# A planner's DMA rates changed: 320 bytes per ns for large rows, 180 for transposes

## The chip, the core and the metric

One core of a Trainium2 chip runs the whole program in one launch. The metric is the device time of one execution in microseconds, as the median of several runs; one execution is also recorded by the hardware profiler.

## What is computed

Attention with a block-causal mask, a dense layer with an ELU, and a mixture of experts with one expert per token:

```python
scores = 1 / sqrt(64) * q @ k.T                  # batch 4, 8 heads, 576 rows, 64 columns
scores = where(row // 64 >= column // 64, scores, -1e9)
x = softmax(scores) @ v                          # regrouped to 2304 tokens x 512
h = x @ w_in                                     # 512 x 2048
x = elu(h) @ w_out                               # 2048 x 512
out = x.copy()                                   # experts: 8, of 512 x 1024 and 1024 x 512
xc = x[x @ w_skip > 0]                           # the other tokens keep x
e = argmax(xc @ w_gate); gate = softmax(xc @ w_gate)[e]
out[those] = xc + gate * (relu(xc @ w1[e]) @ w2[e])
```

## The kernel before

All matrix products that need more precision than one half-precision pass are done as three passes over a high and a low half (f16). The first two chunks of the dense layer use f32 weights that arrive in shuffled form and are rebuilt on VectorE.

**Attention** goes batch by batch (4), in groups of 64-row blocks, by head pairs (4), each row block a unit with five steps: `s_unit` (scores on TensorE), `x_unit` (row maxima on VectorE, exponentials on ScalarE), `h_unit` and `l_unit` (high and low half of the normalised weights, tile `ehl`), and a transpose of `ehl` into `et`, which `pv` multiplies with v on TensorE. The transposes are DMAs issued by SyncE, except for the first two blocks of the first batch, which TensorE transposes (`turn`). `prep_k` and `prep_q` split raw k and q rows and transpose them by DMA into `kt` and `qt`; q is also copied with its halves swapped (`qt<-qt`).

**The dense layer** runs over 9 chunks of 256 tokens (`l1`, `l1a`, `l1b`, `l2`). Its weights come as 32 pieces of 512 KB (`raw_load`, tile `rw`), each rebuilt by three VectorE instructions (`conv`, tiles `twi`, `two`). `post` writes each 128-token tile to the output and to a DRAM scratch `pay_d`, and transposes it by DMA (`x2t`) for the router (`logits`, `route`, `route2`).

**The experts**: weight loads (`load_w`) start when the attention has left its memory (`leave_attention`). They are charged by `rc.call("sp", 0.48, load, [], [pl.key], 1.46, also=left)`, that is with a constant. Tokens are gathered from `pay_d` by GpSimd and transposed by a SyncE DMA (`gather`).

**The order.** Nothing is issued while the program is written down. `Recorder` keeps every instruction as a step with a cost (`_Engine.cost`: busy time on its engine, and for SyncE a second number, the transfer time) and its dependences. `Recorder.order` then plays the whole program through, step by step, on modelled engines, and `issue` emits the instructions in the order of the modelled start times. Of the candidates that are ready on an engine at the earliest time, the one with the lowest record number (`steps[i][3]`) is taken. The modelled times go nowhere else: the chip's engines run their own lists in order and wait on semaphores. One plan reaches from the first load up to the experts; each expert's first tokens and the last ones have small plans of their own, with the same costs. The DMA is one server in the model:

```python
if e == "sp":
    f = max(f, dma_free - 3.0)
...
if e == "sp":
    if len(lanes) >= 8:
        t = max(t, lanes[-8])
    end = max(t + (1.12 if s[1] < 0.6 else 1.3), dma_free) + s[2]
    dma_free = end
    lanes.append(end + 0.9)
    free[e] = t + s[1]
```

Here `s[1]` is SyncE's own issue time and `s[2]` the transfer time; a step that depends on a transfer starts 1.0 us after `end` at the earliest (`LAT["sp"]`).

Of the kernel before, what the change touches and what calls it, by code (L numbers as in the profile page):

```python
# [270 lines left out]
def _count(ap):  # L271
    n = 1
    for _, c in ap:
        n *= c
    return n
# [15 lines left out]
class _Engine:  # L291
# [21 lines left out]
    def cost(self, op, k):  # L313
        e = self.e
        out = k["out"]
        if e == "sp":
            b = _count(out.ap) * mybir.dt.size(out.dtype)
            if op == "dma_start_transpose":
                return max(1.2, b / 290e3 + 0.35), b / 290e3
            run = min(a.ap[-1][1] * mybir.dt.size(a.dtype) for a in (out, k["in_"]))  # L320
            return 0.48, b / 360e3 * (2 if run < 512 else 1)
        n = _count(out.ap[1:])
        sb = all(x.space == bass.MemoryType.SB for x in (out, k.get("in_", out), k.get("in0", out)))
        if e == "pe":
            if op == "transpose":
                return (0.2 if out.dtype == F32 else 0.06), 0.0
            t = n / 2400.0 * (4 if k["lhsT"].dtype == F32 else 1)
            here = out.offset // out.ap[0][0]
            prev, self.rec.last_pe = self.rec.last_pe, here
            return (0.02 if prev == 0 and here == 64 and n < 400 else max(t, 0.01)), 0.0  # L330
        if e == "act":
            aps = any(hasattr(k.get(x), "tensor") for x in ("scale", "bias"))
            return (0.094 if sb else 0.051) + n * 0.833e-3 + 0.093 * (aps + ("accum_out" in k)), 0.0
        if e == "dve":
            if op == "tensor_reduce":
                n = _count(k["in_"].ap[1:])
            aps = any(hasattr(k.get(x), "tensor") for x in ("scalar", "scalar1", "scalar2"))
            x = 1.0
            if op in ("tensor_copy", "tensor_scalar") and sb:
                x = 0.5 if mybir.dt.size(k.get("in_", k.get("in0")).dtype) == 4 else 0.25  # L340
            return 0.069 + n * x / 960.0 + 0.061 * aps, 0.0
        if op == "indirect_dma_start":
            return 1.05, 2.0
        return 0.15, 0.0
# [1602 lines left out]
```

## Time and profile before

| | us |
|---|---|
| median of 3 runs (lowest, highest) | 741.16 (740.03, 742.42) |
| the profiled execution | 738.97 |
| its span on the core | 737.0 |

The profiler records one execution. Busy times are sums over an engine's instructions within the span; a wait is idle time of an engine before an instruction, put down to what released it last. The DMA share is the mean busy share of the core's 16 DMA engines, and can exceed 1 a little. Line L310 is the helper through which all recorded instructions pass, so groups are told apart by their tiles: `out<-in`. PE is TensorE, DVE VectorE, ACT ScalarE, POOL GpSimd, SP or SPq SyncE's queue.

### The profile page before, as it was taken

How to read it: one execution, taken by the hardware profiler on the slowest of the kernel's cores; microseconds unless marked ns; L12 is line 12 of the kernel's file. 1: busy time of each engine (PE TensorE's matmuls, PEld its weight loads, DVE VectorE, ACT ScalarE, POOL GpSimd, SP SyncE). 2: the span in 40 equal slices, each digit the busy share in tenths (PEclk: the TensorE clock that was granted, in tenths of full speed). 3: DMA queues.
4: the chain of work that ended last, by engine and by line, in shares of the span. 5: the costliest groups of instructions: out<-in, count | busy, mean ns of one | idle time of the engine just before them, and what ended most of it. 6: DMA issues, size and time to landing. Idle time of an engine off the chain costs nothing. (4 is left out here: it accounts for less than half of the span.)

```text
span 737.0 us, 17736 instructions
## 1 busy us (share of the span) xinstructions
PE 675.2 (92%) x6665; PEld 464.0 (63%) x6665; DVE 576.2 (78%) x1664; ACT 511.8 (69%) x1090; POOL 84.9 (12%) x122
## 2 busy tenths in 40 slices
PE   4677988999999999989999999999999999998894
PEld 3456633775466666647656667657576777676683
DVE  5897999887999999878969955999688645555662
ACT  5976746899887888667758745766466548585682
POOL 2000000001000100100100000100105034243311
PEclk9989999999999999999999999999999999999998
DMA  9999999799696999899638449826164786999941
GB/s 265 232 260 312 272 285 259 167 166 164 120 194 139 186 179 192 148 177 185 111 66 162 89 70 256 316 78 209 44 200 145 210 173 130 234 240 259 260 131 16
DMA packets 263259, 134.52 MB, mean 183 GB/s; under 512 B 234539, under 2 KB 235573, under 8 KB 262640
## 3 DMA queue, kind: packets, MB, share of 16 engines
q1 hardware_dynamic: 258960, 125.69, 75.0%
q0 software_dynamic: 4192, 7.49, 4.9%
q8 instruction: 57, 0.93, 0.5%
q14 instruction: 50, 0.41, 0.2%
HBM read 74.38 MB, written 12.75 MB: 118 GB/s over the span
## 5 line engine op out<-in xcount | busy, mean ns | idle before, releaser
L310 PE MATMUL h<-xt,win 128*128 128x256 f16 x1344 | 158.5, 273 | 1.6 <-DVE n L310 1.0
L310 PE MATMUL y<-wout,g 128*128 128x512 f16 x672 | 156.5, 381 | 0.0
L310 PEld LDWEIGHTS <-win 128*128 128x128 f16 x1344 | 128.9, 98 | 25.1 <-issue 2.8
L310 PEld LDWEIGHTS <-g 128*128 128x128 f16 x672 | 64.4, 98 | 67.3 <-issue 1.3
L310 ACT ACTIVATE e<-s,mx 128x512 f32<-128x512 f32 (+4 forms) x160 | 82.4, 517 | 26.6 <-DVE mx L310 11.3
L310 ACT ACTIVATE ehl<-e,su 128x512 f16<-128x512 f32 (+4 forms) x160 | 80.5, 550 | 22.4 <-DVE su L310 10.5
L310 DVE SCALAR_TENSOR_TENSOR ehl<-e,su,ehl 128x512 f16<-128x512 f32 (+4 forms) x160 | 81.9, 536 | 10.5 <-ACT ehl L310 10.3
L310 DVE TENSOR_REDUCE mx<-s 128x1 f32<-128x512 f32 (+4 forms) x160 | 74.5, 474 | 6.1 <-PE s L310 5.7
L310 PE MATMUL s<-kt,qt 128*128 128x384 f16 (+5 forms) x384 | 70.1, 310 | 9.9 <-ACT e L310 6.3
L310 PE MATMUL h<-xt,twi 128*128 128x256 f32 x256 | 59.4, 383 | 3.9 <-DVE g L310 2.4
L310 PE MATMUL y<-two,g 128*128 128x512 f32 x128 | 61.3, 618 | 1.3 <-DVE two L310 1.3
L310 PE MATMUL xps<-et,vt 128*64 128x128 f16 (+1 forms) x1440 | 49.5, 218 | 13.8 <-DVE xt L310 2.8
L310 PEld LDWEIGHTS <-vt 128*64 128x64 f16 x1440 | 39.9, 113 | 32.2 <-issue 23.8
L310 ACT ACTIVATE el<-h,col 128x512 f32<-128x512 f32 x56 | 38.2, 682 | 24.5 <-PE h L310 23.6
L310 PEld LDWEIGHTS h<-xt,twi 128*128 128x128 f32 x256 | 47.4, 190 | 10.8 <-DVE g L310 3.0
L310 PEld LDWEIGHTS <-p 128*128 128x128 f16 x984 | 47.0, 99 | 10.2 <-issue 4.1
L310 ACT ACTIVATE g<-el,col 128x512 f16<-128x512 f32 x56 | 40.1, 718 | 18.4 <-DVE el L310 17.9
L310 PEld LDWEIGHTS <-qt 128*128 128x128 f16 (+1 forms) x384 | 28.8, 105 | 28.8 <-issue 11.1
L310 DVE SCALAR_TENSOR_TENSOR g<-el,col,g 128x512 f16<-128x512 f32 x56 | 41.7, 744 | 3.8 <-ACT g L310 3.7
L1506 DVE SCALAR_TENSOR_TENSOR p<-p,n,p 128x1024 f16<-128x1024 f32 x32 | 40.7, 1279 | 4.7 <-ACT p L1505 4.5
L310 DVE SCALAR_TENSOR_TENSOR el<-h,col,el 128x512 f32<-128x512 f32 x56 | 41.7, 745 | 1.3
L310 PEld LDWEIGHTS <-hh 128*64 128x64 f16 (+1 forms) x432 | 28.5, 106 | 19.6 <-DVE hh L310 2.6
(233 smaller groups left out, 1132.3 us busy)
## 6 DMA issues: line engine op xcount, KB each, us to landing
p<-in_moe_w_dram SPq DMA_DIRECT2D x49, 512.0 KB, 5.8
rw<-in_moe_w_in_dram SPq DMA_DIRECT2D x16, 512.0 KB, 7.0
rw<-in_moe_w_out_dram SPq DMA_DIRECT2D x16, 512.0 KB, 5.4
pb<-in_moe_w_dram SPq DMA_DIRECT2D x10, 512.0 KB, 4.5
vflat<-in_v_dram SPq DMA_DIRECT2D x4, 1152.0 KB, 10.2
out_dram<-pay SPq DMA_DIRECT2D x18, 256.0 KB, 2.7
pay_d<-pay SPq DMA_DIRECT2D x18, 256.0 KB, 2.6
raw<-in_k_dram SPq DMA_DIRECT2D x16, 256.0 KB, 4.8
```

The lines of the kernel that those rows point to most:

```text
L310: rec.call(e, time, lambda: getattr(self.real, op)(*args, **kw), reads, writes, dma)
L1506: rc.call("dve", 1.2, lambda: nc.vector.scalar_tensor_tensor(out=half(1), in0=raw.t, scalar=sc, in1=half(0), op0=ALU.mult, op1=ALU.subtrac ...
```

## The change

In `_Engine.cost` the transfer time of a DMA transpose is its bytes at 180 bytes per ns, where it was 290; SyncE's own issue time of the transpose keeps the 290. Another transfer is charged at 320 bytes per ns, where it was 360, if its innermost runs have at least 512 bytes, and at 180, as before, if they are shorter. The constant 1.46 of the expert weights stays.

```diff
@@ -316,9 +316,9 @@
         if e == "sp":
             b = _count(out.ap) * mybir.dt.size(out.dtype)
             if op == "dma_start_transpose":
-                return max(1.2, b / 290e3 + 0.35), b / 290e3
+                return max(1.2, b / 290e3 + 0.35), b / 180e3
             run = min(a.ap[-1][1] * mybir.dt.size(a.dtype) for a in (out, k["in_"]))
-            return 0.48, b / 360e3 * (2 if run < 512 else 1)
+            return 0.48, b / (180e3 if run < 512 else 320e3)
         n = _count(out.ap[1:])
```

## Rows read from the trace of the kernel before

**Rows 1.** The page, part 1: busy time, share of the span, instructions.

```profile
PE 675.2 (92%) x6665; PEld 464.0 (63%) x6665; DVE 576.2 (78%) x1664; ACT 511.8 (69%) x1090; POOL 84.9 (12%) x122
```

**Rows 2.** Stretches: length, busy time (instructions) by engine, PE clock, DMA share, GB/s.

```profile
20.00:140.00 120.00, 98.92 (x691) 62.85 (x690) 107.49 (x287) 82.94 (x189) 1.17 (x5) 0.96 1.04 258
140.00:448.00 308.00, 299.68 (x2989) 199.36 (x2988) 263.29 (x828) 237.60 (x582) 16.77 (x25) 0.99 0.82 148
448.00:600.00 152.00, 150.21 (x1227) 103.93 (x1226) 124.43 (x370) 93.13 (x144) 21.33 (x26) 1.00 0.61 181
600.00:737.00 137.00, 117.30 (x1684) 91.53 (x1681) 70.92 (x151) 86.35 (x158) 41.88 (x28) 0.97 0.76 184
```

**Rows 3.** Stretches of the head: PE, PEld, DVE, ACT, POOL busy; clock, DMA share.

```profile
80.00:100.00 20.00, 18.09 (x101) 9.79 (x100) 20.00 (x44) 13.55 (x28) 0.00 (x0) 1.00 1.16 291
40.00:140.00 100.00, 85.94 (x574) 53.65 (x570) 88.65 (x229) 64.17 (x139) 1.17 (x5) 0.96 1.06 263
```

**Rows 4.** DMA issues, 0 to 140 us: count, KB each, median us to landing.

```profile
rw<-in_moe_w_in_dram SPq DMA_DIRECT2D x16, 512.0 KB, 7.0
...
et<-ehl SPq DMA_TRANSPOSE x11, 5.7
```

**Rows 5.** DMA queues (packets, MB, share) and issues, 408 to 446 us.

```profile
q1 hardware_dynamic: 10540, 2.64, 38.5%
...
et<-ehl SPq DMA_TRANSPOSE x6, 4.3
```

**Rows 6.** Two stretches with loads of expert weights; last columns DMA share, GB/s.

```profile
449.00:453.00 4.00, 4.00 (x41) 3.58 (x40) 2.37 (x6) 1.84 (x3) 0.00 (x0) 1.00 1.01 331
461.00:470.00 9.00, 9.00 (x72) 6.45 (x71) 8.91 (x30) 4.85 (x9) 0.00 (x0) 1.00 1.04 398
```

**Rows 7.** Waits of VectorE, 0 to 140 us: us in total, times, longest.

```profile
DVE twi L310 <- DMA rw<-in_moe_w_in_dram: 6.6, 6, 3.4
...
DVE two L310 <- DMA rw<-in_moe_w_out_dram: 1.5, 2, 1.1
```

**Rows 8.** Timeline of VectorE: start, us, instruction, [idle before it].

```profile
9.21 0.43 DVE L310 TENSOR_SCALAR twi<-rw 128x512 int32<-128x512 int32 x1 [1.02 <-DMA rw<-in_moe_w_in_dram]
...
60.48 0.43 DVE L310 TENSOR_SCALAR twi<-rw 128x512 int32<-128x512 int32 x1 [3.35 <-DMA rw<-in_moe_w_in_dram]
...
61.55 0.68 DVE L310 SCALAR_TENSOR_TENSOR g<-g,h 128x512 f32<-128x512 f32 x1
...
62.75 0.68 DVE L310 SCALAR_TENSOR_TENSOR k<-raw,k 128x512 f16<-128x512 f32 x1
```

**Rows 9.** Waits, 40 to 80 us.

```profile
DVE twi L310 <- DMA rw<-in_moe_w_in_dram: 5.2, 4, 3.4
```

**Rows 10.** Timeline of TensorE behind the wait of 3.35 us.

```profile
62.28 3.72 PE L310 MATMUL h<-xt,twi 128*128 128x256 f32 x16 [0.92 <-DVE g L310]
```

**Rows 11.** Waits of TensorE, 0 to 140 us.

```profile
PE s L310 <- DMA qt<-qt: 1.4, 1, 1.4
```

**Rows 12.** Waits of TensorE, 140 to 600 us.

```profile
PE xps L310 <- DMA et<-ehl: 2.3, 4, 1.1
...
PE s L310 <- DMA qt<-qt: 0.4, 1, 0.4
```

**Rows 13.** Waits of SyncE's queue, 0 to 140 us.

```profile
SPq L310 <- DVE mx L310: 6.5, 3, 5.3
```

**Rows 14.** Waits of TensorE, 600 to 740 us.

```profile
PE hp L310 <- ACTq L1787: 5.7, 4, 2.9
```

**Rows 15.** DMA issues of the whole span, gathers' transposes.

```profile
mxwo<-gp SPq DMA_TRANSPOSE x10, 5.7
```

**Rows 16.** Timeline of TensorE, the last product of attention weights and v.

```profile
446.90 0.86 PE L310 MATMUL xps<-et,vt 128*64 128x128 f16 x24
```

**Rows 17.** Timeline of SyncE, the first loads of expert weights.

```profile
448.97 1.49 SPq L1455 DMA_DIRECT2D p<-in_moe_w_dram  x3
```

**Rows 18.** Stretch in which the experts' weights are prepared.

```profile
520.00:600.00 80.00, 79.19 (x667) 53.69 (x666) 57.94 (x204) 45.28 (x74) 19.14 (x24) 1.00 0.58 155
```

## The prediction

> **What bounds the kernel now.** I read the page first for the engines' shares: TensorE is busy 675.2 of 737.0 us [rows 1], so 61.8 us of idle TensorE is all that a new order can win back. The table of stretches then says where that idle time lies [rows 2]: 20 to 140 us has 120 - 98.92 = 21.1, 140 to 448 has 8.3, 448 to 600 has 1.8, and the experts behind 600 have 19.7 (the rest, about 11, lies before 20 us). From 140 to 600 us the kernel is simply TensorE's work laid end to end. In the first 140 us three things are short at once: from 40 to 140 us VectorE is busy 88.65 of 100 and the DMA share is 1.06, and in the fullest slice, 80 to 100, they stand at 20.00 of 20 and 1.16 [rows 3]. The last places to look were the waits and the DMA rows, because this change touches nothing but the planner's idea of when a transfer ends.
>
> **What the change can and cannot do.** It adds and removes no instruction. The planner writes an order for each engine; its times are thrown away. So a cost matters only where it makes one engine, SyncE among them, take two steps in another order. Three prices move. A transpose goes from bytes/290 to bytes/180: a 256 KB one from 0.90 to 1.46 us, a 512 KB one from 1.81 to 2.91. A large row goes from 360 to 320: a 512 KB piece of the first two weight matrices from 1.46 to 1.64, an 1152 KB block of v from 3.28 to 3.69, a 256 KB write from 0.73 to 0.82. Small rows stay (360/2 is 180). SyncE's own issue time of a transpose, the fixed latencies, the 3 us of backlog, and the 1.46 us which the expert weights carry as a constant all stay.
>
> **Are the new prices nearer to the chip?** I added up what the planner charges for the transfers of a stretch and set it beside the DMA share times the stretch. For 140 to 448 us: transposed attention weights of three batches, 12 head pairs of 1.64 MB, 67.8 us before and 109.2 after; transposes of q and k, 7.08 MB, 24.4 and 39.3; swapped copies of q, 3.5 MB, 9.8 and 11.1; raw q, k, v, 10.6 MB of small rows, 59.0 both; some nine output tiles with a transpose and two writes each, 21.2 and 27.8. The sums are 182 and 246 us. The chip's DMA was busy 0.82 x 308 = 253 us there [rows 2]. For 20 to 140 us, with the counts of that stretch, two of them in [rows 4], less what was issued before 20: 27 weight pieces 39.3 and 44.2, three blocks of v 9.8 and 11.1, raw rows 20.4 both, the transposes 24.6 and 39.6, the small rest about 5.5 both. That is 99.6 and 120.8, against 1.04 x 120 = 125 on the chip [rows 2]. So the old plan believed that a sixth of the DMA was free in the head and 40% in the attention; the new plan sees about what the trace has. A stretch that moved almost nothing but transposes confirms the price: 2.64 MB at 38.5% of 38 us [rows 5] is 180 GB/s of busy time. Its six transposes of attention weights average some 0.40 MB (one 256 KB transpose is in the sum beside them) and landed in a median of 4.3 us [rows 5]; the planner's sum of latency, transfer and hand-over gives 1.3 + 1.37 + 1.0 = 3.7 before and 4.5 after. For large rows the trace is less clear: 398 GB/s at share 1.04 in one stretch, 331 at 1.01 in another [rows 6], so 328 to 383 at a full share, and 320 is low rather than high.
>
> [...]
>
> **The gain, term by term.** What can be won are stalls of an engine at a step that the old plan put too early.
>
> (a) VectorE at pieces of the first weight matrix, 6.6 us in six waits in 0 to 140 us and 1.5 in two at the second matrix [rows 7]. Of the 6.6, 5.2 in four waits lies in 40 to 80 us [rows 9], the largest of them 3.35, which ends at 60.48 [rows 8]; the rest, the larger wait 1.02 of it [rows 8], stands before 10 us, where nothing else is at hand. Behind the 3.35 VectorE had an activation, started at 61.55 [rows 8], for which TensorE waited 0.92 us [rows 10], and a raw k, split at 62.75 [rows 8]; whether either was ready by 57 the rows don't say. Winnable: 5.2 + 1.5 = 6.7 at most, zero at least, because the DMA is full there and the piece comes no sooner. With VectorE busy 88.65 of 100 us a filled stall is worth something, but not all of it reaches TensorE: I take a quarter, 1.7.
>
> (b) TensorE itself at a transfer: 1.4 at swapped q before 140 us [rows 11], then 2.3 at transposed attention weights and 0.4 at swapped q [rows 12], 4.1 in all. A matrix product that stands behind can go first; I take a little under half, 1.9, between zero and the whole.
>
> (c) SyncE, in order too, stops at a transpose whose data is not there, and the loads behind it wait: in 0 to 140 us the waits for the row maxima alone are 6.5 us in three, the longest 5.3 [rows 13]. The change shifts which transfer stands at such a place, and I can't tell to which side: bounds -5.3 to +5.3, the longest single wait, value 0.
>
> (d) The experts have plans of their own, and their gathers' transposes get dearer too. Those stand in SyncE's queue beside weight loads with unchanged cost and are for tokens of the next expert; what ends TensorE's waits there is an engine's branch, 5.7 us in four, not a transfer [rows 14]. Value 0; if loads slip behind such transposes, 0.56 us for each of ten that the longest row counts [rows 15] is a bound of 5.6 on the slow side.
>
> (e) The end of attention at about 447.7 (the last product of attention weights and v starts at 446.90 [rows 16]) releases the memory for the expert weights, whose loads begin two us later, at 448.97 [rows 17]. If the new plan, which charges 64 us more of DMA to the attention, ends it later, the preparation of the experts starts later. From 520 to 600 VectorE, which prepares them, is busy 57.94 of 80 us [rows 18]: 22 us of room. So a slip of a few us costs nothing; without that cover it costs its full length.
>
> Sum: 1.7 + 1.9 = 3.6. The profiled execution took 738.97, its span 737.0; the median of the runs shown is 741.16. I count from the median: **741.16 - 3.6 = 737.5 us**. From the profiled run alone it would be 735.4.
>
> **Rivals.**
> *Same (0.33).* The order changes, the stalls only move. For it: TensorE's waits at transfers are 4.1 us of 61.8, and the head has VectorE, DMA and activations all full, so that reordering leaves each sum as it is. Against it: the old plan is wrong by a sixth in the head, and 3.35 us of VectorE's idle time stands there in one piece. Time: 739 to 743.
> *Slower, by the weight pieces (0.25).* With 0.18 us more for each of 16 pieces of the first matrix, 0.41 for each of three blocks of v and 0.56 for six transposes of q and k, the plan believes the last piece to come 16 x 0.18 + 3 x 0.41 + 6 x 0.56 = 7.5 us later. VectorE then does softmax first, the converted weights come late, and TensorE, which has only attention beside them, stands idle. It decides where the pieces land before the plan's time; rows 6 with 383 GB/s speak for that, the share of 1.06 over 40 to 140 us [rows 3] against it. Half of 7.5 lost gives 745, all of it 748.7.
> *Slower, because transposes are quick (0.05).* If they ran like the large loads of rows 6, the products that use them would stand up to 1.1 us too late in 12 head pairs, 13 us at the end of attention, of which (e) hides most: 742 to 748. [...]
> *Faster (0.37)*, the forecast, 734 to 739. All stalls of (a) and (b) gone would be 6.7 + 4.1 = 10.8: 730.4.
>
> About 2.2 us, 0.3%, is what a measurement here can tell from no change. Faster 0.37, same 0.33, slower 0.30. The range that leaves out no more than 2 in 10 runs from 730, every stall won, to 748, the slow rival nearly whole; the forecast's own is 734 to 739.
>
> **What would show it.** Right: the same number of instructions on each engine; VectorE's wait at weight pieces between 40 and 80 us under 3 us instead of 5.2; TensorE's waits at transfers under 3 instead of 4.1; TensorE's idle time in 20 to 140 us at 18 or less; no more of it from 140 to 600. Wrong: the first product with converted weights clearly later than before and TensorE's idle in the head at 24 or more (the slow rival), or idle time that appears between 448 and 600, or behind 600, where I put nothing: then an order that I held to be covered was not.

## The result and the profile after

The changed kernel takes 748.49 us in the median of six runs (745.74 to 753.53) against 741.79 for the kernel before, measured beside it (six runs, 736.24 to 745.17): a ratio of **1.0141, 95% interval 1.0099 to 1.0182**. This ratio, like every one below, is an estimate over the fast executions (those more than 1.5% above the kernel's fastest are left out) and not the quotient of the two medians beside it, which is 1.0090 here and below differs from the ratio by up to 0.003. Either way the kernel is slower. The forecast was 737.5, and the measured median lies half a microsecond above the top of its range.

The profiled execution took 749.83 us, its span is 748.1, 11.1 more than before. First the page of the changed kernel, part 1:

```profile
PE 682.1 (91%) x6665; PEld 467.0 (62%) x6665; DVE 579.1 (77%) x1664; ACT 510.3 (68%) x1090; POOL 82.9 (11%) x122
```

The instruction counts are those of [rows 1]. TensorE is busy 6.9 us longer and idle 4.2 us longer. The stretches of the changed kernel, with the columns of [rows 2]:

```profile
20.00:140.00 120.00, 98.02 (x611) 63.14 (x610) 107.20 (x283) 80.53 (x183) 0.97 (x4) 0.88 1.02 252
140.00:448.00 308.00, 303.60 (x3054) 200.80 (x3053) 265.82 (x833) 237.16 (x586) 16.31 (x26) 1.00 0.80 152
448.00:600.00 152.00, 145.61 (x1161) 98.44 (x1160) 120.11 (x356) 91.32 (x138) 17.84 (x24) 0.98 0.54 168
```

The granted clock from 20 to 140 us is 0.88 (was 0.96), and from 0 to 20 it was 0.81 (was 1.00); the 256 products `h<-xt,twi` of the dense layer's first chunks take 402 ns in the mean, where they took 383.

Against [rows 2], TensorE's idle time is 22.0 us (was 21.1) from 20 to 140, 4.4 (was 8.3) from 140 to 448, and 6.4 (was 1.8) from 448 to 600. From 140 to 448 TensorE has fewer gaps; the stretch behind it, where nothing was expected, lost 4.6 us. Two milestones, the groups of the attention's last products and of the first products of an expert block (minimum, median and longest duration in ns, first and last start in us), show the same in time:

```profile
L310 PE MATMUL xps<-et,vt x1440: 189/219/316, 21.4 to 449.3; 128*64 128x128 f16 x129, 128*64 128x64 f16 x51
...
L1128 PE MATMUL ahp<-mxt,p x192: 216/219/219, 582.4 to 604.4; 128*128 128x128 f16 x192
```

Before, they start at 447.5 (the group of [rows 16]) and 576.2. So the changed kernel is 1.8 us late at the attention's end, 6.2 late at the first expert block, and 11.1 late at the end.

**What stands between 449 and 582.** The waits of the changed kernel (total, times, longest), whole span:

```profile
PE ns L310 <- DVE cb L310: 4.2, 1, 4.2
...
DVE li L310 <- DMA lst_d<-li,si: 8.1, 4, 5.2
```

And its timeline over the place (start, duration, engine and instruction, [idle before it]):

```profile
454.52 1.83 SPq L1455 DMA_DIRECT2D p<-in_moe_w_dram  x4
456.39 2.07 SPq L1458 DMA_DIRECT2D p<-in_moe_w_dram  x4
458.51 4.42 SPq L1455 DMA_DIRECT2D p<-in_moe_w_dram  x4
463.97 5.25 SPq L1458 DMA_DIRECT2D p<-in_moe_w_dram  x4
...
465.32 0.97 POOL L310 DMA_INDIRECT lst_d<-li,si  x1 [41.43 <-DVE li L310]
471.39 0.97 POOL L310 DMA_INDIRECT lst_d<-li,si  x1 [5.10 <-DMA lst_d<-li,si]
...
470.38 1.21 DVE L1475 TENSOR_REDUCE n<-p 128x1 f32<-128x1024 f32 x1
476.79 0.17 DVE L310 COPY li<-tokid 128x2 f32<-128x2 f32 x1 [5.20 <-DMA lst_d<-li,si]
...
477.83 0.16 DVE L310 CAST cb<-n 128x1 bf16<-128x1 f32 x1
...
478.04 0.16 PE L310 MATMUL ns<-cb,ones 128*128 128x1 bf16 x1 [4.16 <-DVE cb L310]
478.07 5.28 PE L310 MATMUL y<-wout,g 128*128 128x512 f16 x12
```

Read it from the bottom. TensorE stood still 4.16 us for `ns`, a product of 0.16 us that waits for the small tile `cb`. VectorE makes `cb`, and VectorE stood still 5.20 us at a copy of 0.17 us: token numbers into `li`, the buffer of the router's list. `li` is a ring of two, and the buffer was still being read by an indirect scatter into `lst_d`, which GpSimd had issued at 471.39. That scatter and the one ahead of it moved among sixteen 512 KB loads of expert weights, issued from 454.52 to 469.2, and took 5.3 and 5.8 us to land, against a median of 2.8 for all sixteen scatters before. The token numbers don't depend on anything: the planner put the copy far ahead of the gate value that goes into the same buffer, and on an engine in order that makes everything behind it wait for the scatter. Before, the same loads began at 448.97 [rows 17], and the scatters came when they were nearly over; they landed in 2.8 and 2.1 us. GpSimd's timeline of the kernel before:

```profile
474.65 1.22 POOL L310 DMA_INDIRECT lst_d<-li,si  x1 [48.61 <-DVE li L310]
477.67 0.97 POOL L310 DMA_INDIRECT lst_d<-li,si  x1 [1.79 <-DMA lst_d<-li,si]
```

That the loads are what makes the scatter slow is read from these two orders; no run changed the loads alone.

The wait costs twice: twelve `y` products take 2.75 us three times between 457 and 472 of the changed kernel, and 5.28 behind the stall. In 478 to 484 the granted clock is 0.56, after it was 1.00 in 455 to 470. Stretches of the changed kernel:

```profile
455.00:470.00 15.00, 15.00 (x123) 10.51 (x122) 12.89 (x48) 9.46 (x17) 0.97 (x1) 1.00 1.01 383
470.00:478.00 8.00, 3.88 (x30) 2.84 (x29) 2.76 (x12) 2.42 (x4) 0.97 (x1) 0.90 0.97 364
478.00:484.00 6.00, 5.96 (x21) 2.56 (x21) 6.00 (x11) 5.83 (x7) 0.00 (x0) 0.56 0.01 5
```

**Behind 582.** In GpSimd's queue of the changed kernel the scatter of an expert block's result went ahead of the three gathers for the next tokens:

```profile
597.93 1.68 POOL L1168 DMA_INDIRECT out_dram<-o,ah  x1 [7.91 <-DVE lists L310]
599.91 1.10 POOL L310 DMA_INDIRECT gp<-pay_d,lists  x1 [0.31 <-DVE mv L310]
```

Before, the gathers went first:

```profile
590.07 1.18 POOL L310 DMA_INDIRECT gp<-pay_d,lists  x1 [8.42 <-DVE lists L310]
...
596.61 1.65 POOL L1168 DMA_INDIRECT out_dram<-o,ah  x1 [2.49 <-issue]
```

The second expert's first product then waits 4.17 us for a branch where it waited 1.07. TensorE's timeline of the changed kernel, and of the kernel before:

```profile
618.72 1.49 PE L310 MATMUL hp<-mxwo,p 128*128 128x128 f16 x21 [4.17 <-ACTq L1787]
...
608.70 4.20 PE L310 MATMUL hp<-mxwo,p 128*128 128x128 f16 x72 [1.07 <-ACTq L1787]
```

### The profile page after: what moved, and what is told of

Same layout as the page of the kernel before. It is cut to its first block, busy times and chain, and to the rows that moved or that the text cites. A ratio compares the mean times of both kernels' runs of the same rounds, so it can differ in the third digit from the quotient of the medians.

```text
span 748.1 us, 17719 instructions
## 1 busy us (share of the span) xinstructions
PE 682.1 (91%) x6665; PEld 467.0 (62%) x6665; DVE 579.1 (77%) x1664; ACT 510.3 (68%) x1090; POOL 82.9 (11%) x122
## 4 chain that ended last, share of the span: by engine, by line
PE 24%; issue 16%; DMA 9%; DVE 4%; POOL 2%; ACT 1%; POOLq 0%; another core or an unknown queue 0%; DVEq 0%; SPq 0%
PE y L310 11%; PE h L310 9%; DMA gp<-pay_d,lists 4%; PE s L310 2%; PE xps L310 1%; DMA out_dram<-o,gp 1%; DMA x2t<-pay 1%; POOL out_dram L1679 1%; DMA lst_d<-li,si 1%; POOL gp L310 1%; DMA mxt<-gp 1%; DVE ehl L310 1%; DVE el L310 1%; DVE mx L310 0%; DVE g L310 0%
## 5 line engine op out<-in xcount | busy, mean ns | idle before, releaser
L310 PE MATMUL y<-wout,g 128*128 128x512 f16 x672 | 158.5, 384 | 0.5 <-DVE n L310 0.5
L310 PE MATMUL h<-xt,twi 128*128 128x256 f32 x256 | 63.3, 402 | 3.9 <-DVE col L310 3.5
L310 PEld LDWEIGHTS h<-xt,twi 128*128 128x128 f32 x256 | 50.5, 202 | 13.8 <-issue 5.7
L310 PEld LDWEIGHTS <-p 128*128 128x128 f16 x984 | 48.6, 101 | 13.2 <-ACTq L1787 4.4
L310 DVE TENSOR_TENSOR hh<-r,hh 128x256 f16<-128x256 f32 x36 | 14.8, 423 | 35.0 <-ACT hh L310 35.0
```

The costliest lines, as they stand in the source:

```text
L310: rec.call(e, time, lambda: getattr(self.real, op)(*args, **kw), reads, writes, dma)
```

## The experiments

Three theories were stated: **A**, the loss is made by collisions of indirect transfers with bulk transfers behind the attention (and by the lower clock after the stall); **B**, the new prices are too high, so that steps stand too late; **C**, any new order costs about this much, since the old one was one that happened to fit. Ratios are to the kernel before on the same chip, with 95% intervals. The runs are numbered in the order in which they were put on record; an expectation that speaks of "the sixth experiment" means run 6. Runs 1 to 4, 5 to 8, 9 to 11 and 12 to 14 were measured together, each set on one chip. At the end one table splits all profiled spans in three.

### 1. The copies of token numbers moved (run 1)

In each of the eight chunks that have one, the copy of token numbers is put directly ahead of the gate's copy into the same buffer. Only VectorE's list changes; the other engines' lists are those of the changed kernel. The code is laid out on more lines here, and the line that makes the empty list `held` is left out.

```diff
+        o = sorted(done, key=lambda i: (steps[i][6], pos[i]))
+        [(o.remove(i), o.insert(o.index(i + 1), i)) for i in self.held]
+        return o
...
         rc.vector.tensor_copy(li[:, :, 0], tokid[:, 2 * c:2 * c + 2])
+        rc.held.append(len(rc.steps) - 1)
         rc.vector.tensor_copy(li[:, :, 1], gate)
```

> The changed kernel, with one thing moved: each copy of the token numbers into li stands just ahead of the chunk's own gate copy on VectorE, so that it no longer waits on the list scatters of two chunks before; all other lists keep their order. Theory A (the loss comes from two collisions of scatters with bulk transfers, and the lower clock behind them): VectorE's wait of 5.2 us at li and TensorE's 4.2 us at ns are gone, 4 to 7 us shorter than the changed kernel, ratio to the kernel before 1.004 to 1.009. Theory B (the new prices are too high, steps stand too late everywhere): nothing, 1.012 to 1.016. Theory C (any new order costs about this much, whatever it does): a small shift of either sign, within 2 us.

Run 1: 741.25 us, **1.001 [0.9965, 1.0055]**: nearly the whole loss is gone, more than A's range of 1.004 to 1.009; the quotient of the medians is 1.0037. B's and C's ranges are missed. The two waits are gone from the trace, although the collision itself is still there. GpSimd's timeline of this kernel:

```profile
463.96 0.97 POOL L310 DMA_INDIRECT lst_d<-li,si  x1 [41.09 <-DVE li L310]
469.88 0.97 POOL L310 DMA_INDIRECT lst_d<-li,si  x1 [4.95 <-DMA lst_d<-li,si]
```

and its stretches over the place:

```profile
470.00:478.00 8.00, 8.00 (x63) 5.84 (x61) 7.46 (x17) 7.28 (x11) 0.84 (x1) 1.00 0.80 296
478.00:484.00 6.00, 6.00 (x30) 2.69 (x29) 6.00 (x8) 6.00 (x9) 0.00 (x0) 1.00 0.01 3
```

The scatter among the loads is as slow as before the edit (4.95 us until the next one); nothing on VectorE waits for it, TensorE does not stop, and the clock stays at 1.00.

### 2. Gathers first (run 2), and both (run 3)

The result scatters of the first blocks are made to depend on the three gathers, which changes GpSimd's list alone. The lines that collect the gathers' steps in `first_gathers` are left out.

```diff
-        rc.call("pool", 1.05, scatter, [o, ix, out], ["out0"], 2.0)
+        rc.call("pool", 1.05, scatter, [o, ix, out], ["out0"], 2.0, also=first_gathers)
```

> The changed kernel, with the scatters of the two blocks ahead made to stand behind the first three gathers on GpSimd, as they stood in the kernel before; the other engines' lists are the same. Theory A: the gathers run 2 us earlier, their transposes no longer meet the second scatter, TensorE's wait of 4.2 us at the first expert's branch falls to about 1, 3 to 5 us shorter than the changed kernel, ratio 1.007 to 1.011. Theory B: nothing, 1.012 to 1.016. Theory C: within 2 us of the changed kernel.

Run 2: 745.96 us, 1.0102 [1.0066, 1.0137], in A's range. The second expert's wait falls to 1.71 us, `li` still costs 5.0 and `ns` 4.0. The interval overlaps that of the changed kernel, so a gain is not established.

> The changed kernel with both of the former edits. Theory A: their gains add up, 7 to 11 us shorter than the changed kernel, ratio 0.998 to 1.005, and with TensorE's waits at transfers gone perhaps below 1. Theory B: 1.012 or more still. Theory C: 1.008 to 1.018.

Run 3: 740.91 us, 1.0039 [1.0006, 1.0073], in A's range, but not better than the copy alone. The second collision is not a second cause that can be measured. Runs 2 and 3, measured together, differ in the copy's place alone: moving it took 5.05 us off the median.

### 3. The copy moved in the old order (run 5)

> The kernel before, with the copies into li moved as in the first experiment; a control. Its own wait there is 2.3 us, once, and no wait of TensorE hangs on it. If moving the copy mends only the collision of the changed kernel, the ratio is 0.996 to 1.002; if the move is worth as much in any order, 0.985 to 0.992, and the changed kernel's loss has another cause.

Run 5: 737.93 us, 0.9986 [0.995, 1.0021]: the move is worth nothing that can be measured where no scatter meets the loads. So what run 1 took back belongs to the new order.

### 4. One price at a time (runs 6, 7, 4 and 8)

```diff
-                return max(1.2, b / 290e3 + 0.35), b / 290e3
+                return max(1.2, b / 290e3 + 0.35), b / 180e3
```

> The kernel before, with only the transposes at 180 (large rows stay at 360). Theory A: the time goes with the collisions that this order happens to make, not with the price: if the copy into li waits for a scatter as in the changed kernel, 1.008 to 1.015, else 0.995 to 1.005. Theory B (prices too high): most of the loss, 1.008 to 1.014, in many places. Theory C: 1.005 to 1.016. In all of them TensorE waits at transposed attention weights for under 1 us.

Run 6, transposes alone: 739.81 us, 1.0014 [0.9982, 1.0046]. Its attention ends earliest of all (440.6), and then its own `li` copy waits 5.18 us for a scatter, with small waits of TensorE behind it, 3.2 us in four:

```profile
469.39 0.17 DVE L310 COPY li<-tokid 128x2 f32<-128x2 f32 x1 [5.18 <-DMA lst_d<-li,si]
...
476.67 1.35 PE L310 MATMUL y<-wout,g 128*128 128x512 f16 x4 [1.62 <-DVE n L310]
```

All three theories missed: A had 1.008 to 1.015 for an order with this wait, and B and C a loss too. The wait alone does not make the kernel slower than the kernel before; the order's earlier end of the attention makes up for it.

```diff
-            return 0.48, b / 360e3 * (2 if run < 512 else 1)
+            return 0.48, b / (180e3 if run < 512 else 320e3)
```

> The kernel before, with only the large rows at 320 (transposes stay at 290). Theory A: as above, by the collisions; the waits at transposed attention weights stay near those of before, 2 to 5 us. Theory B: a small part of the loss, 1.001 to 1.004. Theory C: 1.005 to 1.016 although the price moves by an eighth.

Run 7, large rows alone: 746.08 us, 1.011 [1.0068, 1.0152], without that wait of TensorE. That is C's range; A's and B's are missed. Its waits in 0 to 140 us:

```profile
PE y L310 <- DVE two L310: 5.4, 5, 1.7
...
DVE two L310 <- DMA rw<-in_moe_w_out_dram: 3.3, 5, 1.2
```

TensorE waited 1.3 us for converted pieces of the second matrix before; the rebuilding of these pieces starts its last step at 133.3 here, at 126.2 before.

> The kernel before, with a transpose charged at 270 bytes per ns instead of 290, and nothing else: a change of 7% in one price, far too small to be right or wrong about the chip. Theory A: it depends on whether the order that comes out of it makes such a collision; the two places tell (wait at li, wait at the first expert's branch). Theory B: a sixth of the loss at most, below 1.003. Theory C: as far from the kernel before as the full change, 3 to 10 us.

Run 4, transposes at 270: 748.98 us, 1.0161 [1.0093, 1.0228], five executions. There is no such collision (the copy into `li` waits 0.2 us), so A does not explain it, and B's limit is passed. TensorE waits 8.7 us at transposed attention weights, but the execution with the profile, 742.62 us, is the fastest of the five and shows little of the loss.

> The kernel before, with a transpose at 240 bytes per ns. Theory B would put it between the fourth experiment and the sixth, in order of price. Theory C puts it anywhere between 1.003 and 1.016, without order: 270 gave 1.016 already. Theory A: TensorE's waits at transposed attention weights fall with the price (8.7 us at 270, 2.5 at 290 and none at 180 are not in order, so this is doubtful); I expect 2 to 6.

Run 8, transposes at 240: 746.02 us, 1.009 [1.0058, 1.0122]; TensorE's waits at transposed attention weights are 3.0 us. The series 290, 270, 240, 180 gives 1, 1.0161, 1.009, 1.0014. That is no price that acts by its size: a price moved by 7% costs as much as the whole change. B fails as a rule for transposes, and so does A, since these two orders lose without the collision; C comes nearest, although run 8 lies between runs 4 and 6, as B had it.

### 5. One price at a time, with the copy moved (runs 9 to 11)

> Only the transposes at 180, with the copies into li moved as in the first experiment. The profile of the sixth experiment ends the attention 7 us before the kernel before did and then stops VectorE 5.2 us at the same copy. Theory A: without that stop the lead is kept, 3 to 7 us below the kernel before, ratio 0.991 to 0.996. Theory C: 0.998 to 1.008, because the lead at that place was only another order of the same work and is given back.

Run 9: 734.74 us, **0.9942 [0.9912, 0.9973]**, as A has it: faster than both kernels. Its two milestones:

```profile
L310 PE MATMUL xps<-et,vt x1440: 189/219/316, 24.3 to 442.9; 128*64 128x128 f16 x129, 128*64 128x64 f16 x51
...
L1128 PE MATMUL ahp<-mxt,p x192: 216/219/219, 569.6 to 590.1; 128*128 128x128 f16 x192
```

> Only the large rows at 320, with the copies moved. In the seventh experiment the copy waited 2.4 us and no wait of TensorE hung on it. Theory A: nothing to win here, 1.007 to 1.012. If moving the copy is good for every order, 0.999 to 1.004.

Run 10: 744.41 us, 1.0072 [1.0044, 1.0099], as A has it. The price of large rows costs something of its own, and not by the collision.

> A transpose at 210 bytes per ns, large rows at 360, the copies moved: a price that the trace bears out nearly as well as 180. Theory A with right prices: near the ninth experiment, 0.991 to 0.998. Theory C: anywhere between 0.995 and 1.012.

Run 11: 740.61 us, 1.003 [1.0005, 1.0054]. A with right prices is missed, C is not: with the copy out of the way, 180 gains and 210 does not.

### 6. Large rows at other prices (runs 12 to 14)

All three have transposes at 180 and the copy moved; run 9 is the same at 360, run 1 at 320.

> The changed kernel with the two copies of token numbers moved, and large rows priced at 300 bytes a ns (transposes stay at 180). Known with the same move: 360 gives 0.9942, 320 gives 1.001. If 320 is too dear a price for large rows (the trace of before had 328 to 383 at a full share), a still dearer one is worse: 1.004 to 1.010. If the loss at 320 is an accident of the one order that it gives, 300 may fall anywhere between 0.994 and 1.006.

Run 12: 745.77 us, 1.0094 [1.0067, 1.0122].

> The same with large rows at 340. A price that acts by its size gives a time between those of 360 and 320: 0.995 to 1.000. An accident of the order: anywhere between 0.994 and 1.006.

Run 13: 746.44 us, 1.0075 [1.0044, 1.0105], outside both.

> The same with large rows at 380, near the 383 that one stretch of the trace of before showed. A price that acts by its size: 0.990 to 0.996, no worse than at 360. An accident of the order: anywhere between 0.994 and 1.006.

Run 14: 737.49 us, 0.996 [0.994, 0.9981].

From 300 to 380 the series is 1.0094, 1.001, 1.0075, 0.9942, 0.996. The two prices at or above the kernel's old one are faster than the kernel before, the three below are not; among these three the time does not follow the price. So neither theory holds alone: the orders at 300 to 340 cost something, and how much does not follow the price. Why these orders are worse is not shown.

### The spans in three parts

From each profiled execution: the start of the attention's last product (part 1), from there to the first product of the first expert block (part 2), and the rest of the span (part 3), in us. A single execution can lie some us from its kernel's median: the one of run 4 lies 6.4 below.

| kernel (transposes / large rows) | part 1 | part 2 | part 3 | span | ratio |
|---|---|---|---|---|---|
| before (290/360) | 447.5 | 128.7 | 160.8 | 737.0 | 1 |
| before, copy moved (run 5) | 443.5 | 128.7 | 165.3 | 737.5 | 0.9986 |
| **changed (180/320)** | 449.3 | **133.1** | 165.7 | 748.1 | 1.0141 |
| copy moved (run 1) | 447.9 | 126.2 | 163.5 | 737.6 | 1.001 |
| gathers first (run 2) | 448.9 | **132.4** | 163.1 | 744.4 | 1.0102 |
| both (run 3) | 444.7 | 126.4 | 163.7 | 734.8 | 1.0039 |
| 180/360 (run 6) | 440.6 | **132.0** | 165.5 | 738.1 | 1.0014 |
| 180/360, copy moved (run 9) | 442.9 | 126.7 | 162.7 | 732.3 | 0.9942 |
| 290/320 (run 7) | 452.2 | 128.7 | 161.4 | 742.3 | 1.011 |
| 290/320, copy moved (run 10) | 452.9 | 128.7 | 161.6 | 743.2 | 1.0072 |
| 270/360 (run 4) | 449.9 | 127.9 | 162.8 | 740.6 | 1.0161 |
| 240/360 (run 8) | 447.3 | 128.7 | 168.3 | 744.3 | 1.009 |
| 210/360, copy moved (run 11) | 449.2 | 126.2 | 161.8 | 737.2 | 1.003 |
| 180/300, copy moved (run 12) | 450.6 | 126.2 | 166.6 | 743.4 | 1.0094 |
| 180/340, copy moved (run 13) | 448.4 | 125.8 | 173.9 | 748.1 | 1.0075 |
| 180/380, copy moved (run 14) | 443.3 | 126.6 | 162.5 | 732.4 | 0.996 |

Part 2 is sharp: the three kernels in which the copy into `li` waits 5 us and TensorE stops behind it (bold; 4.2 and 4.0 us for `ns`, and 3.2 us in four waits in run 6) have 132.0 to 133.1, the other thirteen 125.8 to 128.7. The three pairs with and without the move differ by 6.9, 6.0 and 5.3 us; in the changed kernel that is the stall of 4.16 and the 5.28 - 2.75 = 2.5 at the lower clock.

## Why the prediction was wrong, step by step

**(a) and (b), the waits at transfers: right as to the waits.** VectorE's wait at weight pieces in 40 to 80 us is 2.8 us in one piece (forecast under 3, was 5.2 in [rows 9]), over 0 to 140 us it is 3.1 instead of 6.6, and the 1.5 at the second matrix is gone. TensorE's own waits at transfers are 0.8 us in all (forecast under 3, was 4.1 by the prediction's rows and 4.5 over the whole span):

```profile
PE lp L310 <- DMA x2t<-pay: 0.8, 1, 0.8
```

**The sum of (a) and (b), 3.6 us, fits the transposes' price and not the change.** With 180/360 the attention ends at 440.6 and 442.9, with the kernel before's prices at 447.5 and 443.5: 3.7 us earlier in the mean (445.5 to 441.8), and once the copy is out of the way the kernel takes 0.9942 (737.5 / 741.16 would be 0.995). With large rows alone at 320 it ends at 452.2 and 452.9, 7 us later; with both at 449.3, 447.9, 448.9 and 444.7, in the mean 2.2 later. These are two to four executions each, which differ by up to 4.6 us where TensorE has the same list up to there, so the sizes are rough; the signs rest on the timed ratios. Of the four with both prices, the one that ends earliest (444.7) had a granted clock of 0.99 from 20 to 140 us, the others 0.88 to 0.91. The prediction had read from [rows 6] that 320 "is low rather than high" and gave that no price in the sum. It should have been a term against the change: with transposes at 180 and the copy moved, the runs at 360 and 380 beat the kernel before, those at 300, 320 and 340 don't.

**TensorE's idle time in 20 to 140 us: wrong.** Forecast 18 or less, 22.0. The waits at transfers went and others grew or came, the longest in this stretch behind activations (5.9 us before) and a small step of VectorE (none before):

```profile
PE s L310 <- ACT e L310: 7.4, 8, 1.9
...
PE h L310 <- DVE col L310: 3.5, 1, 3.5
```

That is what the rival *Same* described: the stalls only moved.

**(e), the step that failed.** "A slip of a few us costs nothing" was argued from VectorE's 22 us of room behind 520 us [rows 18]. The slip at the attention's end was indeed small, 1.8 us. But the loads of expert weights moved from 448.97 to 454.52, chunk 5's scatters from 474.65 to 465.32, and so one was laid over the other. In the planner a scatter is a constant (1.05 us of GpSimd and 2.0 until it ends), outside the one server that it has for DMA, so no price of a load can tell it that a scatter among loads takes longer. And the room was of no use to VectorE, which took its list in order: it was idle for 5.20 us at the very moment at which TensorE needed a cast of 0.16 us from it. The prediction named this case as its last sign of being wrong ("idle time that appears between 448 and 600 ... an order that I held to be covered was not"), and gave it no rival with a price. Moving copies of 0.17 us takes it away: 1.0141 to 1.001 in run 1, 1.0102 to 1.0039 from run 2 to run 3, 1.0014 to 0.9942 from run 6 to run 9, and nothing that can be measured in run 5. So the step that was held to cost nothing costs 0.6 to 1.3%.

**How the loss adds up.** From the kernel before with the copy moved (run 5) over runs 9 and 1 to the changed kernel, one thing changes at a time and the ratio goes 0.9986, 0.9942, 1.001, 1.0141. So the price of transposes gains 0.4% (the forecast of 3.6 us is 0.5%), the price of large rows loses 0.7%, and the wait behind the attention loses 1.3%. The other pairs give 0.9% for the large rows (run 10 against 5) and 0.6 and 0.7% for the wait; each difference is uncertain by about 0.5%, so either loss can be the larger. Without the wait (run 1), or without the price of large rows (run 6), the time is again that of the kernel before. By what the price of large rows costs time in the changed kernel stays open.

**A step that was passed over: TensorE's busy time.** The prediction took the 61.8 us of idle TensorE as all that a new order can win back, and so its busy time as fixed. In the changed kernel the same instructions take 682.1 us instead of 675.2, at lower granted clocks in parts of the span (0.81 where it was 1.00 in 0 to 20 us, 0.88 where it was 0.96 in 20 to 140, 0.98 where it was 1.00 in 448 to 600); 2.5 of these 6.9 us lie behind the stall for `ns`. The clock is not the whole loss: over its six timed executions it averages 0.969 for the changed kernel (0.958 to 0.979), and two executions of the kernel before at 0.968, measured beside runs 12 to 14, took 738.3 and 740.3 us. What share the order has in the lower clock of the head was not tested.

**(c) and (d)** had value 0 with bounds of 5.3 and 5.6. SyncE's waits in 0 to 140 us moved to both sides: for row maxima 3.8 us in one (was 6.5 in three, [rows 13]), for rebuilt pieces of the first matrix 13.8 instead of 5.1. Behind 582 us the changed kernel is 4.9 us longer than before, but part 3 varies from 160.8 to 173.9 over kernels whose experts do the same work; run 2 shortened the wait that the traces pointed to, without a measurable gain. Why part 3 is 173.9 in the execution at 180/340 stays open, as does a price for part 3 in general; the wait behind the attention does not account for it.

**The rivals.** *Slower by the weight pieces* named the right sign and the wrong place: the first product with converted weights is earlier than before (44.2 us, was 46.7). Its mechanism is there in run 7, with the large rows' price alone, where TensorE waits 5.4 us for rebuilt pieces, and at 300 (6.9 us); in the changed kernel it waits 1.3, as before. *Slower because transposes are quick* has no support: with the transposes at 180 alone the waits at transposed attention weights fall from 2.5 us to none (run 6) and to 1.1 with the copy moved (run 9), where the kernel gains. That agrees with the 180 GB/s of busy time in [rows 5].

## What to carry to other kernels

A planner with truer prices does not yet give a better order: the greedy one here lost 1.6% for a price moved by 7%, so test a price as a series, and change one price at a time. When a plan shifts a burst of bulk loads, list every small indirect transfer near it and every in-order instruction that reuses its buffer; a copy that depends on nothing should not be moved ahead into a ring of buffers whose old content a DMA still reads. Cover is not a sum over a stretch: ask what the engine will be stopped at when the one it feeds needs its next small result.

## What the runs showed of the hardware

An indirect scatter of two floats a row, median 2.8 us from issue to landing over the kernel before, took 5.3 and 5.8 us among 512 KB loads at a DMA share of 1.01 (455 to 470 us) and 0.97 (470 to 478); one in the kernel before, issued at 297.12 among DMA transposes, took 4.9. One idle stretch of TensorE of 4.16 us, after 15 us at a granted clock of 1.00, was followed by 6 us at 0.56, so this stall cost 2.5 us more than its length; in run 1, without it, the same 6 us have 1.00. And the granted clock in the head is not set by the order alone: with the same list on TensorE it was 0.88 from 20 to 140 us in the changed kernel and in run 1, 0.91 in run 2 and 0.99 in run 3, which makes a single execution's attention end uncertain by some us (449.3, 447.9, 448.9 and 444.7).
